# Attention with forget gates and a gated feed-forward layer on one core: the gate sums of a second pair spread by TensorE, early loads and units reordered

## The chip, the core and the metric

The kernel runs on one core of a Trainium2 chip. A core has TensorE (PE in the profile; PEld is its weight load), VectorE (DVE), ScalarE (ACT), GpSimd (POOL) and SyncE (SP, which here only issues transfers). They run side by side and wait for one another through semaphores. PE reads the on-chip memory SBUF and writes PSUM, whose banks of 128 x 512 float32 are copied out by DVE or ACT. Transfers run on 16 DMA engines; SP issues most of them, POOL those that cast weights to bfloat16 on the way.

The metric is the device time of one execution in microseconds. Shown are the median of several runs, and one profiled execution.

## The reference

Attention over 8 batches of 8 heads, 576 positions and 64 channels, in which a position's weight also falls by the forget gates between it and the query; then a gated feed-forward layer over all 4608 tokens:

```python
def _attn_ref(q, k, v, f):
    scores = scale * np.matmul(q, k.transpose(0, 1, 3, 2))
    log_f = np.log(np.clip(f, 0.0001, 1.0))
    cum = np.cumsum(log_f, axis=-1)
    decay = cum[:, :, :, None] - cum[:, :, None, :]
    scores = np.where(causal, -1000000000.0, scores + decay)
    attn = softmax(scores)
    return np.matmul(attn, v)

def _moe_ref(x, w_gate, w_val, w_out):
    g = x @ w_gate
    silu = g * (1.0 / (1.0 + np.exp(-g)))
    val = x @ w_val
    return silu * val @ w_out
```

q, k and v are float32 of 8 x 8 x 576 x 64, f of 8 x 8 x 576; x is 4608 x 512, the weights are 512 x 1536 twice and 1536 x 512.

## The kernel before

**Pairs.** Two heads make a pair; there are 32 pairs, four to a batch. A pair's queries are cut into 9 blocks of 64, and the two heads lie side by side on the 128 partitions. A pair is worked in two parts: part A (in the code `g` = 0) holds query blocks 0 to 3 and keys up to 256, part B (`g` = 1) blocks 4 to 8 and the rest of the keys. `HEAD` gives the order of the first eight parts: A of pairs 0 to 3, then B of pairs 1, 0, 3, 2. Later pairs go B, then A.

**One part, step by step.** k and q are loaded (L505 for pairs 0 to 3, L424 later), cast to bfloat16 (`kb`, `qb`: L531 to L535, later L452 and L454), transposed on PE (L547, later L468) and copied out (`kt`, `qz`: L562 and L564, later L480 and L482). PE forms the scores (L597) and adds the causal mask (L601). DVE adds the gate sums `cb` and takes the row's minimum (L625); ACT takes the exponential with its row sum (L645); DVE inverts the sum (L659 to L663), and POOL scales to bfloat16 `pk` (L681; ACT sometimes, L679). For pairs 0 to 7 PE transposes `pk` (L711), DVE or ACT copy it out as `pT` (L716); later pairs use a DMA transpose (L694). PE forms the weighted sums with `vt` (L737), the values cast at L782, and DVE or ACT copy them into `xT` (L762), the transposed input of the second layer.

**Gate sums.** DVE forms the running sums of log f for all 64 heads in one tile `t` (L374), and SP writes them to DRAM as `cum_f` (L383). A pair needs its two rows of sums spread over 64 partitions each. Most pairs get that by two broadcast reads of `cum_f` (L431; L514 for parts of pairs 0 to 3). For a few early parts PE spreads them instead: `select` multiplies the tile by a 0/1 matrix `one` (L396, in float32, a 64-row product of 256 columns for part A and 320 for part B), and DVE or ACT copy the result into `cb` (L401). `NSELA` is the number of pairs for which part A is made so, `NSEL` the number for part B:

```python
        for x, a, z, sel in (("A", 0, CUT, NSELA), ("B", CUT, S, NSEL)):
            if p < sel:
                select(p, x, a, z)
                continue
```

**The second layer.** Tokens come in tiles of 256, 256, seven times 512, 256, 128, 128 (`TILES`). For each, PE forms gate and value products (L820), ACT the tanh (L826), DVE two products (L828, L831), PE the output projection (L848); ACT or DVE halve it (L855, L857), and SP writes it (L860). The weights are loaded by POOL in pieces: `wg` and `wv` of 256, 256, 512 and 512 columns (L795), `wo` in three pieces (L799). This layer's products fill PE wherever attention leaves it idle, as soon as tokens of all four pairs of a batch are in `xT`.

**What sets the order.** The kernel is written as some thousands of operations with rough costs, and a planner (`Plan.order`) places them in time at build: among the operations whose inputs are there, the one that can start first, ties by priority. The result is a fixed order of instructions on each engine; on the chip each engine goes through its own in that order and waits where an input is missing. Four things steer it. `STARTUP` lists the first loads in order (f9 the gates, pN k and q, kN and qN those of part B, cN the gate sums, vBC a piece of the values, wgN, wvN, woN weights), and gives them the first priorities. `AHEAD` and `BEHIND` tie a load in that list to the landing of an earlier one in the plan (`BEHIND` for those of POOL). `NUDGE` shifts the priority of named units: aP.G a part of attention, qP a pair's inputs, fT a tile's gate and value products, oT its projection. `COLD` = 25000 tells the planner to double PE's costs in the first 25 us. PSUM has two banks for scores (`sp`), two for transposes and weighted sums (`tx`), four (`gv`) shared by everything else, `select` among it.

Of the kernel before, what the change touches and what calls it, by code (L numbers as in the profile page):

```python
# [199 lines left out]
def kernel(  # L200
# [48 lines left out]

    NHALF = 4  # L250
    NSELA = 4
    NSEL = 1
    LASTA = 3
    CUT = QB * (HI[0] + 1)
    MOST = (("p", 1), ("o", 2), ("f", 3))
    AHEAD = 10
    BEHIND = 4
    BOTH = 8
    LATER = {"DVE": 100}
    SPARE = {"ACT": 400, "DVE": 700}  # L260
# [2 lines left out]
    SOON = 8  # L263
    BACK = 4
    CBACK = 5
    STARTUP = "f9 p0 c0 p2 q0 wg2 v01 q1 k0 wg0 c1 c3 wv2 wv0 k2 v03 v00 v04 c2 wv4 v02 wg4 wg8 q3 v14 q2 v13 p5 p4 wv8 v11 p6 c7 c4 c5 c6 v12 wo4 wo0 wo8 v10 p7"
    HEAD = "00 10 20 30 11 01 31 21"


    NUDGE = "a5.0:0.5 a12.1:1 a13.0:-0.5 a13.1:0.5 a19.0:-2 a22.0:2 a23.0:1 a25.0:0.5 a27.0:-2 a31.0:-2 f6:11.5 f7:2 f8:4 o3:-4 q11:-1 q25:-0.5 q27:1.5 v5:4"  # L270

    WAIT = ""
    ORDER = [(int(u[0]), int(u[1])) for u in HEAD.split()]
# [142 lines left out]
    def load_pair(p):  # L416
# [5 lines left out]
        for name, src, pr in (("k", k, 0), ("q", q, .1)):  # L422
# [4 lines left out]
                (), [(name + "f", p)], (-99 + 3 * p if p < NPB else s - SOON) + pr, dma=1060, after=[sums[p - BACK, 0 if p - BACK >= NPB else 1]] if p >= NPB else [])  # L427
        if p >= NSEL:
            pl.key(("cb", p), "cb", p)
# [64 lines left out]
    def load_parts(p):  # L494
        b, hp = divmod(p, NPB)
        pl.key(("cb", p), "cb", p)
        for name, x, a, z, r, n in parts(p):
# [10 lines left out]
            loads[name, p, x] = pl.op({"ACT" if (name, p, x) == ("k", 0, "A") else "SP": 620 * n}, load, (), [fk], -99 + 3 * p, dma=n * (z - a) * 2)  # L508
        for x, a, z, sel in (("A", 0, CUT, NSELA), ("B", CUT, S, NSEL)):
            if p < sel:  # L510
# [370 lines left out]
    line = []  # L881
    for x in STARTUP.split():
        n = int("".join(c for c in x if c.isdigit()))
# [10 lines left out]
        elif x[0] == "p":  # L894
            line += [loads["k", n], loads["q", n]]
        elif x[0] == "c" and n < NSEL or x[0] == "f":
            continue
# [6 lines left out]
    for n, o in enumerate(line):  # L904
# [3 lines left out]
        if "POOL" in o.engs:  # L908
            o.after.append(line[n - BEHIND])
            o.after += [x for x in line[:n] if "POOL" in x.engs][:-1][-1:]  # L910
# [27 lines left out]

    nudge, leave = ({k: float(v) for k, v in (y.split(":") for y in x.split())} for x in (NUDGE, WAIT))
    for o in pl.ops:  # L940
# [38 lines left out]
```

## Time and profile before

| | us |
|---|---|
| median of 3 runs | 418.1 |
| lowest and highest run | 417.42, 423.13 |
| the profiled execution | 417.56 |
| its span (first to last instruction) | 415.8 |
| PE's first matmul starts | 6.45 |
| PE's last matmul ends | 412.5 |

The granted clock of the profiled execution was 0.999. A row of a timeline gives start, duration, engine, line and operation, output and inputs, shape, the number of merged instructions, and in brackets how long the engine had been idle and who ended that. Starts follow each other closer than durations suggest, since matmuls overlap. A row of the view by stretches gives busy microseconds and instructions of each engine, the granted clock, the mean busy share of the DMA engines, and GB/s.

### The profile page before, as it was taken

Reading aid. Unit: us, or ns where it says so; the run is one execution under the profiler, and the core shown is the slowest. Engines: PE = TensorE matmul, PEld = TensorE weight load, DVE = VectorE, ACT = ScalarE, POOL = GpSimd, SP = SyncE. Lnnn points to the kernel's source line nnn. Section 1 sums busy time; section 2 is a strip of 40 time slices with the busy share of each in tenths; the row PEclk is TensorE's granted clock in tenths of the full one; section 3 lists DMA queues with packets and bytes.
Section 4 is the critical chain, followed back from the end, with each engine's and each line's share of the span. In section 5 each row is a group of like instructions: output and inputs, shape, how many; then the busy total and the mean of one; then the engine's idle time right before and its main releaser. Section 6 shows DMA issues by size and latency. Waiting matters only on the chain.

```text
span 415.8 us, 9975 instructions
## 1 busy us (share of the span) xinstructions
PE 397.3 (96%) x3244; PEld 233.0 (56%) x3296; DVE 325.7 (78%) x1058; ACT 311.9 (75%) x877; POOL 252.6 (61%) x461
## 2 busy tenths in 40 slices
PE   3989899999999999999999999999999999999996
PEld 2657687765555545555555555554554444467674
DVE  5899999988998899788989889889787454565232
ACT  5999899999998999899987998997497322232221
POOL 6798979789677987878698769877626000000000
PEclk9999999999999999999999999999999999999999
DMA  8899999868999999999999999999915501000211
GB/s 184 192 222 226 225 186 261 204 173 211 206 211 210 228 237 208 200 248 207 247 214 204 245 207 247 220 254 203 218 38 129 107 27 50 25 27 25 77 52 53
DMA packets 144005, 71.84 MB, mean 173 GB/s; under 512 B 117904, under 2 KB 131728, under 8 KB 143952
## 3 DMA queue, kind: packets, MB, share of 16 engines
q1 hardware_dynamic: 137856, 66.21, 75.1%
q0 software_dynamic: 5808, 4.72, 7.6%
q8 instruction: 26, 0.43, 0.5%
q10 hardware_dynamic: 288, 0.26, 0.2%
q14 instruction: 27, 0.22, 0.2%
HBM read 46.65 MB, written 9.58 MB: 135 GB/s over the span
## 4 chain that ended last, share of the span: by engine, by line
PE 82%; DMA 8%; DVE 3%; POOL 3%; issue 2%; ACT 1%; ACTq 0%; POOLq 0%; DVEq 0%
PE gv L820 39%; PE gv L848 21%; PE sp L597 9%; PE tx L737 5%; PE tx L468 3%; DMA wo<-in_moe_w_out_dram 3%; POOL pk L681 2%; PE sp L601 2%; DMA kf<-in_k_dram 2%; DMA pT<-pk 2%; PE gv L711 2%; DMA qf<-in_q_dram 2%; DVE t L625 1%; PE gv L396 1%; PE tx L547 1%
## 5 line engine op out<-in xcount | busy, mean ns | idle before, releaser
L625 DVE CUSTOM_DVE_ANT_0 t<-sp,cb 128x512 f32<-128x512 f32 (+7 forms) x288 | 131.0, 475 | 15.1 <-PE sp L601 10.1
L681 POOL TENSOR_SCALAR pk<-e,lr 128x128 bf16<-128x128 f32 (+3 forms) x191 | 101.0, 532 | 47.5 <-DVE tm L625 20.2
L820 PE MATMUL gv<-xT,wv 128*128 128x512 bf16 (+2 forms) x563 | 109.6, 325 | 0.6
L820 PE MATMUL gv<-xT,wg 128*128 128x512 bf16 (+2 forms) x565 | 109.6, 325 | 0.7
L828 DVE SCALAR_TENSOR_TENSOR th<-th,gv 128x512 f32<-128x512 f32 x108 | 73.9, 684 | 44.8 <-ACT th L826 44.3
L848 PE MATMUL gv<-wo,hh 128*128 128x512 bf16 (+1 forms) x420 | 103.5, 373 | 1.5 <-DMA wo<-in_moe_w_out_dram 0.5
L826 ACT ACTIVATE th<-gv 128x512 f32<-128x512 f32 x108 | 63.9, 591 | 45.0 <-PE gv L820 43.1
L645 ACT ACTIVATE e<-t,tm 128x448 f32<-128x448 f32 (+4 forms) x160 | 88.7, 556 | 7.3 <-DVE tm L625 6.8
L831 DVE TENSOR_TENSOR hh<-th,gv 128x512 bf16<-128x512 f32 x108 | 73.6, 684 | 6.6 <-PE gv L820 3.8
L597 PE MATMUL sp<-kt,qz 128*128 128x384 bf16 (+6 forms) x316 | 72.6, 294 | 3.4 <-DVE tm L625 2.0
L645 ACT ACTIVATE eo<-t,tm 128x384 f32<-128x384 f32 (+3 forms) x128 | 71.0, 556 | 4.1 <-DVE tm L625 2.3
L681 POOL TENSOR_SCALAR pk<-eo,lr 128x384 bf16<-128x384 f32 (+3 forms) x127 | 67.4, 531 | 7.8 <-DVE lr L663 6.9
L820 PEld LDWEIGHTS <-wg 128*128 128x128 bf16 x576 | 49.1, 98 | 34.8 <-DMA wg<-in_moe_w_gate_dram 0.4
L820 PEld LDWEIGHTS <-wv 128*128 128x128 bf16 x576 | 49.2, 98 | 34.4
L848 PEld LDWEIGHTS <-hh 128*128 128x128 bf16 x444 | 40.0, 98 | 38.6 <-DMA wo<-in_moe_w_out_dram 0.7
L601 PE MATMUL sp<-mask,ident 128*128 128x64 bf16 x288 | 48.6, 197 | 0.0
L597 PEld LDWEIGHTS <-qz 128*128 128x128 bf16 x320 | 31.1, 101 | 20.7 <-issue 0.8
L855 ACT ACTIVATE ot<-gv 128x512 f32<-128x512 f32 (+1 forms) x34 | 19.6, 580 | 28.7 <-PE gv L848 28.5
L601 PEld LDWEIGHTS <-ident 128*128 128x128 bf16 x288 | 27.5, 101 | 13.8 <-issue 2.3
L452 POOL TENSOR_SCALAR qb<-qf 72x1024 bf16<-72x1024 f32 x28 | 29.2, 1041 | 5.3 <-DMA qf<-in_q_dram 2.2
L737 PE MATMUL tx<-pT,vt 128*64 128x320 bf16 (+4 forms) x448 | 29.6, 266 | 1.5 <-DVE pT L716 1.0
L645 ACT ACTIVATION_READ_ACCUMULATOR e<-t,tm 128x1 f32 x160 | 30.6, 191 | 0.0
(68 smaller groups left out, 385.3 us busy)
## 6 DMA issues: line engine op xcount, KB each, us to landing
out_dram<-ot SPq DMA_DIRECT2D x35, 256.0 KB
vf<-in_v_dram SPq DMA_DIRECT2D x32, 256.0 KB
kf<-in_k_dram SPq DMA_DIRECT2D x28, 288.0 KB
qf<-in_q_dram SPq DMA_DIRECT2D x28, 288.0 KB
cb<-cum_f SPq DMA_DIRECT2D x56, 144.0 KB
wo<-in_moe_w_out_dram POOLq DMA_DIRECT2D x3, 512.0 KB, 11.5
vf<-in_v_dram SPq DMA_DIRECT2D x8, 128.0 KB
wv<-in_moe_w_val_dram POOLq DMA_DIRECT2D x2, 512.0 KB, 8.2
```

The source lines that it names most:

```text
L452: eng[e].tensor_scalar(dst, src, -scale, 1.0, op0=ALU.mult, op1=ALU.mult)
L597: nc.tensor.matmul(sp[:, o:o + z - a], qz[:, i, :, :].rearrange("p h r -> p (h r)"), kt[:, a:z], start=True, stop=not last or p >= MFROM)
L601: nc.tensor.matmul(sp[:, o - QB:o], ident, mask, start=False, stop=True)
L625: nc.vector.tensor_tensor_reduce(out=pl.buf(tk)[:, a:z], in0=pl.buf(sk)[:, o:o + z - a], in1=pl.buf(("cm", p))[:, i, :] if own else pl.buf ...
L645: nc.scalar.activation(pl.buf(ek)[:, :L], pl.buf(tk)[:, :L], AF.Exp, bias=pl.buf(("tm", p, g))[:, 0, i:i + 1], scale=-1.0, accum_out=pl.bu ...
L681: eng[e].tensor_scalar(dst, src, r, 1.0, op0=ALU.mult, op1=ALU.mult)
L737: nc.tensor.matmul(xo[r, 0:QB * n], vt[:, c, 2 * hp + h, :], pT[:, a:a + n, 64 * h:64 * h + 64], start=(c == 0), stop=(c == nch - 1))
L820: nc.tensor.matmul(pl.buf(bk)[:, j * n:j * n + n], wt[:, ko, fc * P:fc * P + P], xT[:, ko, x0:x0 + n], start=ko == 0, stop=ko == KD - 1)
L826: pl.op({"ACT": 487}, lambda e, u=u: nc.scalar.activation(pl.buf(("th", t, u)), pl.buf(("wg", t, u)), AF.Tanh, scale=0.5), [("wg", t, u)], ...
L828: pl.op({"DVE": 605}, lambda e, u=u: nc.vector.scalar_tensor_tensor(pl.buf(("th", t, u)), pl.buf(("th", t, u)), 1.0, pl.buf(("wg", t, u)), ...
L831: pl.op({"DVE": 605}, lambda e, u=u: nc.vector.tensor_mul(pl.buf(("hh", t, u)), pl.buf(("th", t, u)), pl.buf(("wv", t, u))), [("u", t, u), ...
L848: nc.tensor.matmul(pl.buf(bk)[:, 0:z - a], hh[:, (fc % nf) * n + ms * P:(fc % nf) * n + ms * P + P], wo[:, fc, a:z], start=fc == 0, stop=f ...
```

## The change

Pair 1's part B joins the parts whose gate sums are spread by PE; the list of first loads has a new order; POOL's loads are tied in the plan to a load one place further back; and the priorities of other units are shifted.

```diff
-    NSEL = 1
+    NSEL = 2
...
-    BEHIND = 4
+    BEHIND = 5
...
-    STARTUP = "f9 p0 c0 p2 q0 wg2 v01 q1 k0 wg0 c1 c3 wv2 wv0 k2 v03 v00 v04 c2 wv4 v02 wg4 wg8 q3 v14 q2 v13 p5 p4 wv8 v11 p6 c7 c4 c5 c6 v12 wo4 wo0 wo8 v10 p7"
+    STARTUP = "f9 p0 p2 v01 wg2 k0 wv2 q1 q0 wg0 c3 wv0 v03 c0 v00 c2 wv4 k2 wg4 q3 c1 v04 wg8 q2 v02 v13 p5 wv8 p4 c5 p6 v11 v14 v10 c4 p7 c6 v12 c7 wo0 wo4 wo8"
...
-    NUDGE = "a5.0:0.5 a12.1:1 a13.0:-0.5 a13.1:0.5 a19.0:-2 a22.0:2 a23.0:1 a25.0:0.5 a27.0:-2 a31.0:-2 f6:11.5 f7:2 f8:4 o3:-4 q11:-1 q25:-0.5 q27:1.5 v5:4"
+    NUDGE = "a5.0:-1 a12.1:1 a14.1:-2 a16.0:2 a17.1:1 a18.0:1 a22.0:3.5 a24.1:2 a25.1:1.5 a27.0:-1 f4:-4 f5:2.5 o2:-2 o3:-11.5 o5:-10 o6:-6 o7:-12 q18:-1.5 q19:-2 q21:-3"
```

What it does to the instructions: PE has one matmul more (L396, 320 columns, for pair 1), DVE one copy more (L401), SP two broadcast reads fewer (L514). On PE the first 18 or so microseconds of work keep their order. From there, the B scores of pairs 1 and 0 are interleaved with the weighted sums and `pk` transposes of part A, which stood behind most of them before; and gate products of the first token tile are spread among the scores of pairs 3 and 2. On POOL the issue of wv's first piece directly follows that of wg's; the issues of wv and wg of columns 512 to 1023 stand one behind the other and earlier; the first two pieces of `wo` are issued together, the first rows first. The cast of pair 0's and 1's k of part B moves from POOL to ACT, where it stands ahead of the copy of `qz` and of pair 1's exponentials; two copies of `pT` move from DVE to ACT, one of `kt` from ACT to DVE. Behind that the order of units differs all through the kernel, with the same work on PE; the last 30 groups of PE's work are the same in shape and order.

## The prediction

> **What bounds the kernel now.** I read the page's totals first, then its chain of waits.
>
> ```profile
> span 415.8 us, 9975 instructions
> PE 397.3 (96%) x3244; PEld 233.0 (56%) x3296; DVE 325.7 (78%) x1058; ACT 311.9 (75%) x877; POOL 252.6 (61%) x461
> PE 82%; DMA 8%; DVE 3%; POOL 3%; issue 2%; ACT 1%; ACTq 0%; POOLq 0%; DVEq 0%
> ```
>
> TensorE (PE) is busy 397.3 of 415.8 us and holds 82% of the chain. Nearly every product of the kernel is computed there in both versions, so a new order can only win back time in which PE stands still or runs slowly. The view of busy time by stretches says where that is (columns: stretch and length, then busy us of PE, PEld, DVE, ACT, POOL):
>
> ```profile
> 6.40:25.40 19.00, 16.89 (x103) 11.26 (x105) 14.62 (x64) 15.93 (x56) 14.16 (x27) 1.00 1.03 200
> 25.40:29.30 3.90, 2.94 (x38) 1.87 (x37) 3.90 (x14) 3.84 (x14) 3.81 (x8) 1.00 1.16 257
> 29.30:60.00 30.70, 28.28 (x335) 23.20 (x335) 29.16 (x92) 28.48 (x75) 25.73 (x42) 1.00 1.17 211
> 60.00:100.00 40.00, 39.06 (x426) 26.97 (x431) 35.74 (x134) 38.20 (x108) 36.12 (x62) 1.00 0.88 210
> 100.00:400.00 300.00, 297.69 (x2211) 160.09 (x2252) 234.34 (x742) 218.71 (x618) 167.52 (x296) 1.00 0.82 167
> 400.00:412.60 12.60, 12.48 (x141) 9.56 (x139) 4.13 (x6) 3.88 (x8) 0.00 (x0) 1.00 0.12 44
> 412.60:415.80 3.20, 0.00 (x0) 0.00 (x0) 0.00 (x0) 0.36 (x1) 0.00 (x0) 0.80 0.47 164
> ```
>
> Length minus PE busy is PE's idle time: 2.11 us up to 25.4, 0.96 up to 29.3, 2.42 up to 60, 0.94 up to 100, and 2.31 in all the 300 us behind that. Before 6.4 PE has nothing to work on, behind 412.6 only the last output leaves. All idle time between is 8.86 us, 2.1% of the span. That caps what reordering alone can bring. The timeline of PE shows the second reserve, slow running:
>
> ```profile
> 16.03 1.43 PE L396 MATMUL gv<-t,one 64*128 64x320 f32 x2
> 17.39 0.82 PE L711 MATMUL gv<-ident,pk 128*128 128x128 bf16 x6
> 18.00 0.42 PE L597 MATMUL sp<-kt,qz 128*128 128x256 bf16 x1
> 18.22 0.26 PE L601 MATMUL sp<-mask,ident 128*128 128x64 bf16 x1
> 18.77 0.72 PE L547 MATMUL tx<-ident,qb 80*128 80x80 bf16 x8
> 19.29 0.84 PE L711 MATMUL gv<-ident,pk 128*128 128x128 bf16 x6
> 21.11 0.26 PE L597 MATMUL sp<-kt,qz 128*128 128x64 bf16 x1 [0.98 <-DVE qz L564]
> ...
> 25.05 0.24 PE L601 MATMUL sp<-mask,ident 128*128 128x64 bf16 x1
> 25.10 0.51 PE L597 MATMUL sp<-kt,qz 128*128 128x448 bf16 x1
> 25.45 0.19 PE L601 MATMUL sp<-mask,ident 128*128 128x64 bf16 x1
> ...
> 27.30 0.35 PE L737 MATMUL tx<-pT,vt 128*64 128x256 bf16 x4 [0.77 <-DVE pT L716]
> 29.34 1.03 PE L820 MATMUL gv<-xT,wg 128*128 128x256 bf16 x8
> 32.45 1.04 PE L820 MATMUL gv<-xT,wv 128*128 128x256 bf16 x8
> 39.09 1.05 PE L820 MATMUL gv<-xT,wg 128*128 128x256 bf16 x8
> 61.32 0.27 PE L597 MATMUL sp<-kt,qz 128*128 128x256 bf16 x1
> 61.43 0.19 PE L601 MATMUL sp<-mask,ident 128*128 128x64 bf16 x1
> 72.42 1.04 PE L848 MATMUL gv<-wo,hh 128*128 128x512 bf16 x3 [0.49 <-DMA wo<-in_moe_w_out_dram]
> ```
>
> From start to start a 256-column score takes 0.22 us at 18.00 and 0.11 at 61.32, and the mask matmul drops from 0.24 to 0.19 between 25.05 and 25.45. So PE runs at half speed until about 25.2 us, while the granted-clock column reads 1.00 throughout: that column does not show this slowness.
>
> **The change, part by part.** The profiled execution took 417.56 us, its span of 415.8 and 1.76 around it; the median of the three runs is 418.1, 0.5 above. I sum against 417.56.
>
> *Gate sums of pair 1, part B, on PE.* One matmul L396 of 320 columns is added: 17.39 − 16.03 = 1.36 us at the slow speed, half of it (an estimate, by 0.22 against 0.11) at the full one. In the new order it stands at about 19.0, behind the first four transposes of the row at 18.77. There PE has the hole of 0.98 that ends at 21.11, which waits for DVE's qz copies and not for PE. The copies keep their place (DVE has lost a pT copy to ACT and gained a kt copy and the new cb copy). So 1.36 − 0.98, or **+0.4**; −0.2 if PE warms early, +1.4 if the hole stays.
>
> ```profile
> 17.49 0.49 DVE L401 COPY cb<-gv 128x320 f32<-128x320 f32 x1
> 14.16 2.39 SPq L514 DMA_DIRECT2D cb<-cum_f  x4
> 13.51 0.72 POOL L535 CAST kb<-kf 128x640 bf16<-128x640 f32 x1 [0.48 <-DMA kf<-in_k_dram]
> 12.43 0.61 POOL L782 CAST vt<-vf 128x512 bf16<-128x512 f32 x1 [3.78 <-DMA vf<-in_v_dram]
> 22.71 0.17 DVE L663 RECIPROCAL lr<-lr 128x4 f32<-128x4 f32 x1
> 23.86 0.47 POOL L681 TENSOR_SCALAR pk<-eo,lr 128x256 bf16<-128x256 f32 x1
> 25.66 0.36 POOL L681 TENSOR_SCALAR pk<-e,lr 128x128 bf16<-128x128 f32 x1
> 26.57 0.80 POOL L795 DMA_DIRECT2D wv<-in_moe_w_val_dram  x1
> 29.00 0.81 POOL L795 DMA_DIRECT2D wg<-in_moe_w_gate_dram  x1
> wv<-in_moe_w_val_dram POOLq DMA_DIRECT2D x2, 512.0 KB, 8.2
> wg<-in_moe_w_gate_dram POOLq DMA_DIRECT2D x2, 512.0 KB, 9.7
> ```
>
> The sum's copy out of PSUM is one more of 0.49 us; on DVE it fits beside the pT copies handed to ACT. Two of the four cum_f broadcasts that SP issues from 14.16 go away, half of 2.39 us of SP's time. SP had no later work waiting on PE's path there: nothing gained.
>
> *Order from 19 to 29.3.* The changed order puts the weighted sums (L737) of pairs 0 to 2 between the B scores instead of behind them, and the qb transposes of pairs 2 and 3 ahead of the first gate. Walking it with the rows, all at the slow speed: the gate sum from 19.0 to 20.4, six transposes (18.00 − 17.39 = 0.61) to 21.0, four more (half of 19.29 − 18.77) to 21.3, and the first B scores there (before: 21.11). PE then waits for POOL. The last scalings of pair 3 are released by the reciprocal, which ended at 22.9 before (22.71 + 0.17); afterwards two weight issues of 0.80 stand among them, so pk is whole at 22.9 + 0.47 + 0.47 + 0.80 + 0.80 + 0.36 = 25.8 (before: 25.66 + 0.36 = 26.0). PE, through two score groups and three of weighted sums and transposes by then, arrives at about 24.9. With 0.3 more for qb, the first gate starts near 29.5, and a qb transpose group is done that stood behind gates before. The new waits are about 1.3 us, the old ones 0.96 (0.77 of it for pT at 27.30) and 2.11 − 0.98 beside the hole; the difference is 0.8, and with less than half of it taken, since the walk holds guesses, I count **−0.3**; bounds −1.5 and +1.5, the new waits gone or doubled.
>
> *Loads.* wv of the first 256 columns goes out directly behind wg, ahead of POOL's first cast: +0.8 us of issue on POOL, which stood idle for 3.78 us until 12.43 anyway. The two issues in the walk of POOL above are wv and wg of 512 columns: at about 23.8 and 24.6, against 26.57 and 29.00. With 9.7 us to land, wg is there at 34.3 instead of 38.7. In the kernel before the fifth gate group starts at 39.09, right after that landing, and no gate stands between the one at 32.45 and that; afterwards it can start at 34.5. So PE has filler where it waited. Of the 2.42 idle up to 60 I take **−0.7**; bounds −2.4 (all of it) and +1.5 (the gate queued at 34.5, with the scores behind it on PE, finds its weight late). wo for the first rows is now issued first: the wait of 0.49 at 72.42 can go, **−0.2**, bounds −0.5 and +1.
>
> *The retuned priorities behind 100 us.* They reorder a stretch with 2.31 idle in 300. **0**, bounds −1 and +2. The last 30 groups on PE are the same in shape and order, other buffers apart: 0.
>
> Sum: +0.4 − 0.3 − 0.7 − 0.2 = −0.8. From 417.56 that gives 416.8; a median over runs lay 0.5 above the profile, of which I add 0.2: **417.0**.
>
> **Page against row.** PE's busy share is 16.89 of 19.00 us while slow. The Trainium skill ("TensorE: Matmul & The Clock Gate", Part 1) says that one busy window of about 3.4 us releases the full clock. The trace disagrees: far more than that went by here. Its Part 4 says that transposes don't count as busy for that gate; that fits, since transposes and 64-row sums fill much of this stretch, and it speaks against the change: the dense run of scores from 21.11 to 25.45 is now broken up by sums, transposes and weighted sums.
>
> **Rivals.** *Late warming.* PE stays slow past 25.2, up to the first gate. Price: the 2.94 busy up to 29.30 doubles, 2.94, and idle time takes up 0.96: +2.0 on the forecast, so 419.0. For it: PE's own stretch of B scores is thinner. Against: waits on pk and qb hide part of it. It decides if the mask matmul still takes 0.24 at 27. *Loads collide.* DMA share is 1.03 to 1.17 already. wv beside the early loads delays kf, whose cast (13.51, after 0.48 of waiting) moves to ACT ahead of its exponentials; or wg lands after 34.5. Price: some 1 to 1.5 us, 418.3. The Trainium skill ("DMA: Bandwidth & Descriptors", Issuing engines are not separate DMA queues) says that all queues share 16 engines and interleave; by that the early wv is paid by others; the share of over 1 agrees. *It goes better.* Idle up to 100 us halves and the clock keeps its time: 0.4 − 1.0 − 1.6 − 0.5 = −2.7, so 415. *Nothing comes of it.* The sums were hidden, gaps move but don't shrink: 417.7. *PE turns cold again* between 29 and 60. If half speed held for 9 us of the 28.28 busy there, +9 us, 426, slower by over 2%. From there PE's busy share is 92% (28.28 of 30.70) or more, and the rows at 61.32 and 61.43 are fast: unlikely.
>
> **How the numbers follow.** Forecast 0.40, nothing 0.12, late warming 0.18, loads 0.15, better 0.11, cold again 0.04. The unknown bounds behind 100 us go into the range: 414.4 to 420.8 leaves out the cold case and the tails of the two ends. Two per cent, 8.4 us, is about what a measurement can tell from no change. Faster by that would need nearly all the 8.86 idle: 0.01. Slower: the cold case and a stall not foreseen, 0.05. Within: 0.94.
>
> **What would show it.** Right: L396 six times, the new one near 19 with the hole gone; first gate at 29.3 to 29.8; a fifth gate group near 34.5; PE idle under 1.8 between 29.3 and 60; the mask matmul at 0.19 by 26. Wrong: 0.24 still at 28, a wait on kf or wg before 35, or idle over 4 us between 100 and 400.

## The result and the profile after

| | before | after |
|---|---|---|
| median of 15 runs, us | 418.46 | 423.04 |
| lowest and highest, us | 417.42, 470.43 | 420.8, 425.79 |
| ratio, 95% interval | | 1.0097 (1.0074 to 1.0121) |
| profiled execution, its span, us | 417.56, 415.8 | 422.14, 420.4 |

The 470.43 is a single disturbed run and doesn't move the median. The changed kernel is about 1% slower, and the interval leaves no doubt of the sign. The forecast was 417.0, and 423.0 lies above the predicted range of 414.4 to 420.8. The two profiled executions differ by 4.6 us, as the medians do, so they can be compared stretch by stretch.

The page of the kernel after, its span, PE's totals and the group of output projections:

```profile
span 420.4 us, 10002 instructions
PE 402.4 (96%) x3298; PEld 233.1 (55%) x3298; DVE 326.9 (78%) x1059; ACT 312.1 (74%) x876; POOL 253.1 (60%) x462
L848 PE MATMUL gv<-wo,hh 128*128 128x512 bf16 (+1 forms) x444 | 106.4, 373 | 2.9 <-DMA wo<-in_moe_w_out_dram 2.9
```

PE's share is 96% as before, and this tells nothing. The last line does: PE stood still for 2.9 us in front of projections, all of it for `wo`. PE's count of 3298 equals its weight loads; the page before has 3244 matmuls for 3296 loads. So 52 matmul records are missing there, and each leaves a hole that looks like idle time. That bears on a reading below.

The view by stretches of the kernel after (stretch, length, then busy us of PE, PEld, DVE, ACT, POOL; granted clock, DMA share, GB/s):

```profile
6.40:19.00 12.60, 10.78 (x55) 6.66 (x55) 7.41 (x32) 8.95 (x30) 6.68 (x12) 1.00 1.12 213
19.00:25.40 6.40, 6.40 (x48) 4.19 (x48) 5.79 (x30) 5.78 (x21) 5.38 (x13) 1.00 1.06 200
...
60.00:80.00 20.00, 16.73 (x186) 12.97 (x184) 16.14 (x54) 15.90 (x45) 15.80 (x28) 1.00 1.12 226
80.00:100.00 20.00, 19.92 (x228) 12.60 (x224) 19.23 (x77) 19.24 (x58) 17.67 (x33) 1.00 0.65 165
100.00:200.00 100.00, 100.00 (x814) 53.25 (x811) 91.50 (x330) 92.33 (x278) 81.43 (x142) 1.00 1.05 219
200.00:300.00 100.00, 100.00 (x773) 52.14 (x772) 85.77 (x289) 86.25 (x252) 73.18 (x130) 1.00 1.05 216
300.00:400.00 100.00, 99.82 (x664) 54.05 (x663) 59.25 (x132) 43.75 (x104) 17.67 (x33) 1.00 0.31 73
```

The same view of the kernel before, in the three stretches that differ most:

```profile
6.40:19.00 12.60, 12.24 (x73) 8.24 (x74) 8.97 (x39) 10.64 (x38) 7.85 (x14) 1.00 0.90 190
19.00:25.40 6.40, 4.64 (x34) 3.02 (x33) 5.65 (x26) 5.29 (x18) 6.31 (x14) 1.00 1.29 218
...
60.00:80.00 20.00, 19.23 (x229) 14.93 (x231) 18.72 (x66) 18.92 (x51) 17.44 (x29) 1.00 1.07 235
```

Up to 19 us PE is idle for 1.82 us instead of 0.36, from there to 25.4 not at all instead of 1.76, and between 60 and 80 for 3.27 instead of 0.77. From 100 to 400 it hardly rests after the change (0.18 in 300 us). What is lost by then can't be won back.

PE's timeline of the kernel after (start, duration, operation; in brackets the idle time before it and who ended it):

```profile
16.16 0.72 PE L547 MATMUL tx<-ident,kb 128*128 128x128 bf16 x5 [1.46 <-ACT kb L531]
...
17.79 1.43 PE L396 MATMUL gv<-t,one 64*128 64x320 f32 x2
...
20.91 1.43 PE L396 MATMUL gv<-t,one 64*128 64x320 f32 x2
...
26.45 0.26 PE L601 MATMUL sp<-mask,ident 128*128 128x64 bf16 x1
...
27.74 0.40 PE L711 MATMUL gv<-ident,pk 128*128 128x128 bf16 x4 [0.49 <-POOL pk L681]
...
28.11 0.19 PE L601 MATMUL sp<-mask,ident 128*128 128x64 bf16 x1
...
32.13 1.04 PE L820 MATMUL gv<-xT,wg 128*128 128x256 bf16 x8
...
37.45 1.04 PE L820 MATMUL gv<-xT,wg 128*128 128x256 bf16 x8
...
72.10 1.04 PE L848 MATMUL gv<-wo,hh 128*128 128x512 bf16 x4 [1.97 <-DMA wo<-in_moe_w_out_dram]
...
76.75 1.02 PE L848 MATMUL gv<-wo,hh 128*128 128x512 bf16 x4 [0.95 <-DMA wo<-in_moe_w_out_dram]
```

The new sum stands at 20.91. (One float32 product shows as two records: L396 has 12 of them, so six products.) The transposes at 16.16, which came at 14.63 before, wait for a cast on ACT. The first gate group starts at 32.13 instead of 29.34, yet the fifth at 37.45 instead of 39.09. Then come the two waits for `wo`, where there was one of 0.49.

If both traces are lined up at equal matmul work done on PE (counted in columns, a float32 product four times, in the order of the instructions), the run after lies behind the run before by:

```
at time after, us    20     25     32     51     69     73     77     90    410
behind, us          1.8   -0.1    2.1   -0.7    1.2    3.3    3.4    3.6    3.9
```

The rest up to 4.6 is the added sum, which this count takes as work. So the start loses some 2 us, the early gates win them back for a while (0.4 behind at 45, ahead at 51, 0.5 behind at 62), and what counts at the end is lost between 51 and 77: 2.2 from 69 on, where PE waits for `wo`, and 1.9 ahead of that in small pieces, with no wait over 0.35 among them.

Where the two kinds of waits come from: ACT's timeline of the kernel after, and POOL's issues of `wo` after and then before:

```profile
15.37 0.74 ACT L531 ACTIVATE kb<-kf 128x640 bf16<-128x640 f32 x1 [2.06 <-DMA kf<-in_k_dram]
```

```profile
60.33 1.55 POOL L799 DMA_DIRECT2D wo<-in_moe_w_out_dram  x2
...
68.84 0.80 POOL L799 DMA_DIRECT2D wo<-in_moe_w_out_dram  x1
```

```profile
56.39 0.80 POOL L799 DMA_DIRECT2D wo<-in_moe_w_out_dram  x1
59.91 0.79 POOL L799 DMA_DIRECT2D wo<-in_moe_w_out_dram  x1
...
65.32 0.80 POOL L799 DMA_DIRECT2D wo<-in_moe_w_out_dram  x1
```

k of part B is there about 1.9 us later: its cast started on POOL at 13.51 before.

`wo` comes in three pieces, and the order of `STARTUP` tells which issue is which. From issue to landing the view of the tile `wo` gives 7.1 us at the least, 11.5 in the middle and 12.5 at the most before, and 11.2, 11.7 and 15.6 after. Before it reads wo4 wo0 wo8, so the issue at 56.39 is the second piece (7.1 us to landing), and the first piece, which the first projection begins with, goes out at 59.91 and is there 12.5 us later, at 72.42. After the change it reads wo0 wo4 wo8: the first piece goes out at 60.33 and is there 11.8 us later, at 72.10, hardly sooner than before. What makes the first wait is PE: it gets to the first projection at 72.10 − 1.97 = 70.13, before at 72.42 − 0.49 = 71.93. The second wait comes from the new order of the pieces: the second now goes out behind the first, at about 61.1, and is there 15.6 us later, at 76.75.

The order of the instructions held this already. By the plan's own times, at which it places an operation when the kernel is built, the first projection stood 12.0 us behind the issue of its piece before the change, and 8.7 us behind it after.

### The profile page after: what moved, and what is told of

It is laid out like the page before. It is cut to its first block, busy times and chain, and to the rows that moved or that the text cites. A ratio compares the mean times of both kernels' runs of the same rounds, so it can differ in the third digit from the quotient of the medians.

```text
span 420.4 us, 10002 instructions
## 1 busy us (share of the span) xinstructions
PE 402.4 (96%) x3298; PEld 233.1 (55%) x3298; DVE 326.9 (78%) x1059; ACT 312.1 (74%) x876; POOL 253.1 (60%) x462
## 4 chain that ended last, share of the span: by engine, by line
PE 79%; DMA 8%; ACT 5%; POOL 4%; issue 1%; DVE 1%; ACTq 0%; SPq 0%; POOLq 0%; DVEq 0%
PE gv L820 38%; PE gv L848 21%; PE sp L597 8%; PE tx L737 5%; DMA wo<-in_moe_w_out_dram 4%; POOL pk L681 3%; PE tx L468 3%; DMA kf<-in_k_dram 3%; DMA pT<-pk 2%; ACT e L645 2%; PE sp L601 2%; PE gv L711 1%; ACT eo L645 1%; PE gv L396 1%; ACT qz L480 0%
## 5 line engine op out<-in xcount | busy, mean ns | idle before, releaser
L820 PE MATMUL gv<-xT,wg 128*128 128x512 bf16 (+2 forms) x576 | 111.3, 326 | 0.0
L820 PE MATMUL gv<-xT,wv 128*128 128x512 bf16 (+2 forms) x576 | 111.3, 326 | 0.0
L848 PE MATMUL gv<-wo,hh 128*128 128x512 bf16 (+1 forms) x444 | 106.4, 373 | 2.9 <-DMA wo<-in_moe_w_out_dram 2.9
L681 POOL TENSOR_SCALAR pk<-eo,lr 128x512 bf16<-128x512 f32 (+3 forms) x128 | 68.2, 533 | 10.7 <-DMA pT<-pk 6.9
L597 PE MATMUL sp<-kt,qz 128*128 128x448 bf16 (+5 forms) x320 | 73.0, 294 | 0.5 <-DVE tm L625 0.3
L645 ACT ACTIVATE eo<-t,tm 128x256 f32<-128x256 f32 (+3 forms) x128 | 71.1, 555 | 2.5 <-DVE tm L625 1.5
L855 ACT ACTIVATE ot<-gv 128x512 f32<-128x512 f32 (+1 forms) x28 | 16.1, 578 | 29.7 <-PE gv L848 29.7
## 6 DMA issues: line engine op xcount, KB each, us to landing
wo<-in_moe_w_out_dram POOLq DMA_DIRECT2D x3, 512.0 KB, 11.7
```

Of the source, the lines that this page charges most:

```text
L597: nc.tensor.matmul(sp[:, o:o + z - a], qz[:, i, :, :].rearrange("p h r -> p (h r)"), kt[:, a:z], start=True, stop=not last or p >= MFROM)
L645: nc.scalar.activation(pl.buf(ek)[:, :L], pl.buf(tk)[:, :L], AF.Exp, bias=pl.buf(("tm", p, g))[:, 0, i:i + 1], scale=-1.0, accum_out=pl.bu ...
L681: eng[e].tensor_scalar(dst, src, r, 1.0, op0=ALU.mult, op1=ALU.mult)
L820: nc.tensor.matmul(pl.buf(bk)[:, j * n:j * n + n], wt[:, ko, fc * P:fc * P + P], xT[:, ko, x0:x0 + n], start=ko == 0, stop=ko == KD - 1)
L848: nc.tensor.matmul(pl.buf(bk)[:, 0:z - a], hh[:, (fc % nf) * n + ms * P:(fc % nf) * n + ms * P + P], wo[:, fc, a:z], start=fc == 0, stop=f ...
```

## The experiments

Two explanations were set against each other: that the time is lost at the waits for `wo`, because PE takes its projections in a fixed order and these now stand too early (W); and that it is lost in the first 25 us, through the early load of wv and the late warming, and carried to the end (S). The added sum is a third, smaller part. Each edit keeps the plan and moves only the operations named in the finished order, unless said otherwise. The first four kernels were measured beside 10 runs of the kernel before (median 418.31), the last four beside 34 (418.28).

**wo earlier.** On the changed kernel, the issues of `wo` are moved ahead by 6 us of the plan's time.

```diff
-        for o in pl.order():
+        shift = {loads["wo", c].n: -6000 for c in (0, 4, 8)}
+        for o in sorted(pl.order(), key=lambda o: (o.start + shift.get(o.n, 0), o.n)):
```

> The changed kernel with one thing moved: POOL issues the three wo loads some 6 us of plan time earlier (the first two near 55 us instead of 60.33). Theory W (the loss is made by PE standing in front of its first projection for wo, 1.97 us at 72.10 and 0.95 at 76.75, after everything before was caught up): both waits go, the span falls by 2.0 to 2.9 us, from about 420.4 to 417.5 to 418.4; ratio to the kernel before about 1.003. Rival L (the transfer engines are full, so an earlier wo only delays k and v loads of later pairs): the wait moves to kb, qb or vt on POOL and the time falls by less than 0.8 us. Rival S (the loss is made in the first 30 us, by slow running and the added sum): no change beyond 0.5 us.

Measured: 425.28 us, ratio 1.0169 (1.0136 to 1.0202), so slower than the change itself. W had forecast 417.5 to 418.4 for the span, and that failed; the sign of rival L came true, with the wait moved to `vt`. The waits for `wo` are gone, but another is there. POOL's timeline of this kernel, then PE's, then its stretches:

```profile
53.88 1.55 POOL L799 DMA_DIRECT2D wo<-in_moe_w_out_dram  x2
...
68.72 0.61 POOL L782 CAST vt<-vf 128x512 bf16<-128x512 f32 x1 [5.85 <-DMA vf<-in_v_dram]
```

```profile
69.94 0.61 PE L711 MATMUL gv<-ident,pk 128*128 128x128 bf16 x4 [4.79 <-POOL pk L681]
...
71.05 1.89 PE L820 MATMUL gv<-xT,wg 128*128 128x256 bf16 x8
```

```profile
66.00:70.00 4.00, 0.06 (x1) 0.06 (x2) 0.00 (x0) 0.00 (x0) 1.28 (x3) 0.89 1.16 265
70.00:74.00 4.00, 4.00 (x31) 3.18 (x32) 2.15 (x5) 1.57 (x4) 3.37 (x7) 0.50 0.76 173
```

The DMA engines are full here (a mean busy share of 1.16). SP issues this `vf` at 56.08, as in the changed kernel (56.04), yet its cast starts 4.4 us later than there (64.34): `wo` takes its time on the engines. The cast stands on POOL ahead of the scalings `pk`. PE stands still for 4.79 us, and then runs at a clock of 0.50, a gate group in 1.89 instead of 1.04. Issuing `wo` sooner doesn't cure the waits; it moves them to another transfer, at a higher price.

**wv later.** On the changed kernel, the issue of wv's first piece goes back to just ahead of wv's second, past POOL's first casts.

```diff
+        seq = pl.order()
+        late = seq.pop(seq.index(loads["wv", 2]))
+        seq.insert(seq.index(loads["wv", 0]), late)
```

> The changed kernel with the first wv load put back: its issue on POOL stands directly ahead of the second wv load (near 18 us) instead of directly behind the first wg load at 6.16. All theories: k of part B lands near 13.5 instead of 15.3, ACT's wait of 2.06 us for it falls below 0.5, and PE's wait of 1.46 us at 16.16 goes. Theory W: the time hardly moves (0 to 1.0 us less), as this lag had been caught up by 50 us in the changed kernel and wo's landing sets the place of the first projection. Rival S: the whole 1.5 us is won, 2 us if PE also warms sooner, so 418.4 to 419.

Measured: 421.88 us, ratio 1.0096 (1.0062 to 1.0131); against the changed kernel's 1.0097 no gain that these runs can tell. In its profile the wait for k is gone, and PE then meets the same missing `wo` earlier. PE's timeline of this kernel:

```profile
69.15 1.04 PE L848 MATMUL gv<-wo,hh 128*128 128x512 bf16 x3 [0.42 <-DMA wo<-in_moe_w_out_dram]
...
74.45 1.02 PE L848 MATMUL gv<-wo,hh 128*128 128x512 bf16 x4 [1.59 <-DMA wo<-in_moe_w_out_dram]
```

The projections run 3.0 and 2.3 us earlier than after the change, and still wait. That is far from S's 418.4 to 419, which speaks against S as the whole cause. This profile alone would say less: its execution was the fastest of the five (420.3), and its span of 418.5 is 1.9 us shorter than after the change.

**Both edits together.**

> Both moves of the two kernels ahead of this one. Theory W: as with wo early alone or up to 1 us better, about 417 to 418, so about the kernel before or 0.2% above. Rival S: wo adds nothing to the other, 418.4 to 419. If neither load matters, 422.

Measured: 425.44 us, ratio 1.0159 (1.0127 to 1.0191). As with `wo` alone, `vf` is late: POOL's timeline of this kernel, then PE's.

```profile
69.58 0.61 POOL L782 CAST vt<-vf 128x512 bf16<-128x512 f32 x1 [6.19 <-DMA vf<-in_v_dram]
```

```profile
70.81 0.61 PE L711 MATMUL gv<-ident,pk 128*128 128x128 bf16 x4 [5.47 <-POOL pk L681]
```

**The second sum, planned anew.** The kernel before with `NSEL = 2` and nothing else; the planner sets a new order.

```diff
-    NSEL = 1
+    NSEL = 2
```

> The kernel before with NSEL = 2 alone, planned anew; loads list, BEHIND and priorities as before. Theory W: the added sum costs 0.4 to 1.4 us of PE near 19 us and no more, 418.5 to 420, unless the new plan happens to place the first projection ahead of wo's landing, which a wait at the first L848 over 1 us would show. Rival S: 1.5 us or more from slow running between 25 and 29, with the mask matmul at 0.24 or more at 27.

Measured: 422.41 us, ratio 1.0092 (1.0057 to 1.0128). PE's timeline of this kernel:

```profile
46.72 0.43 PE L468 MATMUL tx<-ident,qb 72*128 72x72 bf16 x8 [2.13 <-POOL qb L452]
...
50.41 0.60 PE L597 MATMUL sp<-kt,qz 128*128 128x512 bf16 x2 [1.01 <-DVE tm L625]
```

That is outside W's 418.5 to 420. It is as slow as the whole change, but through other waits, which neither kernel has, and not through S's slow running: the mask matmul takes 0.19 from 25.97 on. The sum's own price can't be read from a plan that was made anew.

**The projection later.** A projection of 128 tokens is made of three groups of four matmuls, one for each piece of `wo`. On the changed kernel, the first tile's first projection moves back on PE: its first group to just ahead of where the second stood, its second to just ahead of the first group of the next 128 tokens (the expectation says the second). `wo` is issued as in the changed kernel.

```diff
+        proj = {(o.writes[0][2], o.writes[1][1]): o for o in pl.ops if o.writes[0][:2] == ("op", 0)}
+        for o, then in ((proj[0, 4], proj[0, 8]), (proj[0, 8], proj[1, 4])):
+            seq.remove(o)
+            seq.insert(seq.index(then), o)
```

> The changed kernel with the loads left alone and two matmul groups of the first projection moved back on PE: its first four f-blocks from behind the kb transposes at 69.71 to where its second four stood (76.75), its second four to just ahead of the second projection's second four, some 5 us of PE work later. Theory W (in-order waiting of PE for wo while other work stands behind it): both wo waits (1.97 and 0.95) go or fall below 0.5 together, PE does the scores, transposes and gates behind them meanwhile; span 417.5 to 418.4, ratio to the kernel before 1.002 to 1.005, and no run with a mean granted clock under 0.998. Rival D (up to 80 us everything waits on loads: take one wait away and vt or kb of the next pairs is late instead): the gain stays under 1 us, ratio 1.007 or more, and the new wait is named POOL or DMA in front of L711, L468 or L737.

Measured: 419.64 us (11 runs), ratio 1.0037 (1.0020 to 1.0054), an interval wholly below that of the change. PE's timeline of this kernel, and its stretch from 60 to 80:

```profile
72.94 1.03 PE L848 MATMUL gv<-wo,hh 128*128 128x512 bf16 x3
...
76.79 1.89 PE L848 MATMUL gv<-wo,hh 128*128 128x512 bf16 x7
```

```profile
60.00:80.00 20.00, 18.85 (x212) 14.44 (x212) 18.40 (x66) 18.19 (x50) 18.09 (x32) 1.00 1.10 229
```

No bracket stands behind the projections now, PE is busy for 18.85 of 20 us instead of 16.73, and the span falls from 420.4 to 417.5, by the two waits of 1.97 and 0.95. That carries W: 0.6% of the 0.97% are these waits, to within some 0.3% by the two intervals. Of W's conditions only the one on the clock failed: one run of the eleven reads 0.996.

**Both late: projection and wv.**

> That and the first wv load put back behind, as in the earlier run with wv late, whose profiled span was 418.5 with wo waits of 0.42 and 1.59. Theory W: both gains add, 2.0 us off 418.5, span 416 to 417.3, ratio 0.997 to 1.001: as fast as the kernel before. Rival D: 418 to 419, ratio 1.003 to 1.007.

Measured: 418.84 us (12 runs), ratio 1.0017 (1.0001 to 1.0033). That falls between the two forecasts (W up to 1.001, D from 1.003). Beside the projection alone it is 0.2% less, with intervals that overlap, so the second gain isn't shown. PE's timeline of this kernel has a new wait, for a weight that the gates now need sooner than it lands:

```profile
37.42 1.05 PE L820 MATMUL gv<-xT,wg 128*128 128x256 bf16 x8 [1.23 <-DMA wg<-in_moe_w_gate_dram]
```

**The sum's own price.** The kernel before, its plan kept, with the product of L396 for part B of pair 0 done twice into the same bank.

```diff
+            for _ in range(2 if part == "B" else 1):
+                nc.tensor.matmul(pl.buf(bk)[:, 0:z - a], w, pl.buf("fa")[0:BH, a:z], start=True, stop=True)
```

> The kernel before, same plan and order, with its one 320-column gate sum (L396 at 16.03) computed twice in a row. It measures what an added sum costs on PE near there and nothing else. If the 0.98 hole at 20.1 absorbs it and the rest of the 25 us keeps pace: 0.3 to 0.5 us, ratio 1.001. If all of it stays: 1.36, ratio 1.003. If it is caught up later, as the lag of the changed kernel was between 40 and 55 us: 0, ratio 1.000. If it delays warming by a window of the clock gate: 2 us or more, ratio 1.005, and the mask matmul reads 0.24 or more at 26.5.

Measured: 419.0 us, ratio 1.0024 (1.0009 to 1.0038), which is 1.0 us. PE's timeline of this kernel (its lines lie one further down):

```profile
16.91 2.50 PE L397 MATMUL gv<-t,one 64*128 64x320 f32 x4
...
23.07 0.26 PE L598 MATMUL sp<-kt,qz 128*128 128x64 bf16 x1 [0.99 <-DVE qz L565]
...
30.66 0.24 PE L602 MATMUL sp<-mask,ident 128*128 128x64 bf16 x1
```

The hole in front of the first B scores doesn't take this sum up: it stays at 0.99 and comes 2 us later. Of these 2 us, 0.9 were there ahead of the sum (16.91 against 16.03), and 1.07 are the second product (2.50 − 1.43). The second product stands ahead of the transposes of `qb`, and the hole waits for copies of these. In the changed kernel the new sum stands between them (20.91, with transposes at 20.53 and 22.89), so its price there may be lower. The 1.0 us (0.4 to 1.6 by the interval) need not be the product alone: the mask matmul still takes 0.24 at 30.66, so in this execution PE ran slowly some 5 us longer than before. Whether the second product made that, one trace can't tell.

**wv early, alone.** The kernel before, its plan kept, with the issue of wv's first piece right behind that of wg's.

```diff
+        early = seq.pop(seq.index(loads["wv", 2]))
+        seq.insert(seq.index(loads["wg", 2]) + 1, early)
```

> The kernel before, same plan, with its first wv load issued directly behind the first wg load, as in the changed kernel, and nothing else. Expected by all: the second piece of k lands 1.5 to 2 us later (13.5 to 15.3) and POOL's cast of it with it, so PE waits 1 to 1.5 us near 15 to 16. If a delay of the start stays to the end: ratio 1.002 to 1.004. If gates fill it in by 55 us and the first projection waits for wo anyway (0.49 at 72.42): ratio 1.000 to 1.001.

Measured: 418.43 us, ratio 1.0006 (0.9981 to 1.0031). POOL's timeline of this kernel:

```profile
15.14 0.72 POOL L535 CAST kb<-kf 128x640 bf16<-128x640 f32 x1 [1.61 <-DMA kf<-in_k_dram]
```

k is there 1.6 us later than the 13.51 before, nearly as late as after the change. Over all ten profiled executions its cast starts between 14.60 and 15.37 in the four kernels with the early wv, and between 13.42 and 14.73 in the six without. So the early wv delays k by about 1 us on the average, and single executions differ by as much. In the profiled execution the span is longer by 1.3 us; in the medians hardly anything of that is left. What the early wv costs in time stays open between nothing and about 0.3%.

## Why the prediction was wrong

**The step that failed** is the last of the loads: "the wait of 0.49 at 72.42 can go, −0.2, bounds −0.5 and +1". The wait grew to 1.97 and got a second of 0.95 behind it, +2.4 in place of −0.2. The step looked only at which piece of `wo` is issued first, and took the order for a time of landing. The first piece went out at 60.33 instead of 59.91 and was there at 72.10 instead of 72.42, so the first projection got it hardly sooner. The step did not ask where that projection stands on PE in the new order: it is reached at 70.13 instead of 71.93, with less work done. Nor did it ask what becomes of the second piece, which went out first before and now lands so late that PE waits for it too. Where the projection stands and in which order the pieces go could both be had from the order of instructions. Moving the projection alone took back 0.6%.

**The added sum** was counted at +0.4, by letting the hole of 0.98 take it up. Done twice on the kernel before, it costs 1.0 us (0.24%, between 0.4 and 1.6 us), and the hole stays. After the change the hole is gone, but PE had come there later by its 1.46 of waiting, so the copies may have had time enough without the sum; no run separates the two. The term was too low by up to 0.6; the bounds of −0.2 to +1.4 hold it.

**The early loads.** "Idle up to 60, −0.7" was right in kind: the fifth gate group came 1.6 us sooner, and the run after was ahead by 0.7 at 51 us. But it started 2 us behind, and PE's idle time between 29.3 and 60 was 2.20, not under 1.8 (before: 2.42). The lead was short, and PE then stood still for `wo`. A gain ahead of a late transfer is kept only if the transfer lands sooner too.

**wv behind wg at no cost** was argued from POOL's idle 3.78 us. POOL was indeed free; the DMA engines weren't (a share of 1.12 up to 19 us, before 0.90). k slipped by 1.9 us in this kernel and by 1.6 with wv moved alone, by about 1 on the average of the executions. This was the rival in which loads collide, right in its mechanism (0.15; its 418.3 left out everything at 72). Its share of the loss is not settled.

**Late warming** was half right. The mask matmul still took 0.26 at 26.45 and 0.19 at 28.11, so PE ran slowly up to 27 or so instead of 25.2, which belongs to the lag of 2.1 at 32 us. Its price at the end is not the 2.0 of that rival: in the profiled execution with the sum done twice PE ran slowly up to 30.66, longer than after the change, and that execution took 419.03, 1.5 above the profiled one before, with a second product and a late k in it as well. The first gate came at 32.13 instead of the forecast 29.5; 0.7 of its delay against before (2.8 − 2.1) is work that the new order puts ahead of it.

**Order from 19 to 29.3** was put at −0.3; PE lost instead, as the lag goes from −0.1 at 25 us to 2.1 at 32. The walk had PE wait for POOL and then go on to the first gate. PE waits for `pk` (0.49 at 27.74), but then five times more: 0.13 for POOL, and 0.17, 0.61, 0.05 and 0.15 for DVE and ACT, the last four already behind the forecast 29.5; and it runs slowly for longer.

**Priorities behind 100 us** at 0 was right for a reason that was not: "2.31 idle in 300" were mostly holes left by missing matmul records: 41 of the 52 are missing there, and 41 idle pieces for which the trace names no other engine make up 2.18 of the 2.31. After the change, with all 3298 recorded, PE's idle time there is 0.18. So the cap of 8.86 us on what reordering could win was too high by about two.

The sum as it should have been: +2.4 for the waits at `wo` and up to +1.0 for the added sum; what is left of the 4.6, 1.2 or more, is the delayed k, late warming and order, which these runs don't tell apart. None of the kernels tried is faster than the one before; of those built on the change the nearest, with projection and wv late, is at 1.0017.

## What to carry to other kernels

When an order changes, count for every piece of a late transfer two things in the new one: when it is issued, and how much work the consumer's engine has in front of its first use; a gain ahead of it is kept only if the transfer moves too. Where the DMA engines are full, moving one load forward delays another, so first try to move the use back. And before idle time is added up into a reserve, compare the counts of matmuls and weight loads: missing records look like idle time.

## What the runs showed of the hardware

**One long wait costs twice.** In the kernel with `wo` earlier, PE stood still for 4.79 us and then ran at a granted clock of 0.50, though busy without a break. A later stretch of that kernel's view:

```profile
75.00:76.00 1.00, 1.00 (x8) 0.73 (x7) 0.00 (x0) 0.46 (x2) 0.00 (x0) 0.54 0.09 27
```

The row from 70 to 74 said 0.50, and here it is still 0.54. From the restart at 69.94 that makes about 6 us at half speed, 3 us lost beside the 4.79. In the kernel with both loads moved it was about 4 us, from 70.81 to 75. The Trainium skill ("TensorE: Matmul & The Clock Gate", Part 1) says that the clock is halved after an idle window of about 3.4 us and released after a busy one of the same length, by windows that run freely; the fall agrees, and the return took between one and two such windows.

**The clock can fall without a long wait.** In the kernel with projection and wv late, PE was fast early and then fell back. A row of its PE timeline, and then its stretches:

```profile
16.16 0.80 PE L396 MATMUL gv<-t,one 64*128 64x320 f32 x2
```

```profile
19.00:21.00 2.00, 1.55 (x12) 0.64 (x10) 1.81 (x11) 2.00 (x10) 2.00 (x6) 1.00 1.12 168
21.00:23.00 2.00, 1.03 (x12) 0.74 (x13) 1.97 (x8) 1.48 (x5) 2.00 (x5) 0.85 1.32 245
23.00:25.00 2.00, 2.00 (x16) 1.16 (x14) 1.75 (x7) 2.00 (x6) 2.00 (x5) 0.50 1.20 224
```

The sum takes 0.80 at 16 us, against 1.43 at 17.79 after the change. PE is then busy for only about half of 21 to 23 us, in pieces with no wait over 0.62 between them, and the clock goes to 0.50. That the thin work is the cause is likely, but one execution doesn't show it. With wv late alone, PE's order is the same up to that sum, yet the mask matmul takes 0.26 at 16.04, where it takes 0.19 here. So the speed of the first 25 us differs between executions by more than the order explains, and a walk through that stretch at one fixed speed can't be good to better than a microsecond or two. The granted-clock column shows this fall; it does not show the slowness at the very start, where it reads 1.00.
